# A gated attention and token-mixing MLP kernel: MLP stretches of one length, o sums kept outside PSUM, one pool of seven banks

## The chip, the core and the metric

The kernel runs on one core of one Trainium2 chip. The core has TensorE (PE in the profile, with PEld for its weight loads), VectorE (DVE), ScalarE (ACT), GpSimd (POOL) and SyncE (SP, which here issues the DMAs). TensorE writes only to PSUM, which has eight banks of 128 partitions x 512 float32 values. GpSimd does not read PSUM in this kernel: what it works on is first copied out by ScalarE or VectorE. The metric is the device time of one execution in microseconds (us), the median of several runs.

## What is computed

```python
g = sigmoid((x * gate_w).sum(-1, keepdims=True))
# attention: 32 heads of 20, one shared k and v
q = (x @ wq) as (32 heads, 2048, 20); k = x @ wk; v = x @ wv
p = softmax(q @ k.T * 20 ** -0.5)
a = concat(p @ v over the heads) @ wo
# token-mixing MLP, applied across the 2048 tokens
h = layernorm(x)                     # (2048, 640)
u = gelu(h.T @ w1 + b1)              # (640, 1728)
b = (u @ w2 + b2).T                  # (2048, 640)
return g * a + (1 - g) * b
```

x is 2048 x 640 in float32. Matrix products are computed with a high and a low part of each operand (hi x hi, hi x lo, lo x hi), so each product counts three matmuls.

## The kernel before

The program is written out in one order by hand: the scheduler is manual, so the order in the code is the order on each engine. It has a front part (layer norm, projections, about 96 us), a lead (the first seven tiles of the W1 product, mixed with the first row-max scores), the **main phase** that the change touches, and a tail of 24 o visits with the rest of the output product.

**Units and visits.** Attention runs over 32 row groups n (four blocks of 512 query rows x eight groups of four heads). Each has 16 units, one for each block kb of 128 keys. For a unit, four *scores* (`qk`, line 696: two halves b of the PE's rows x two heads pr) make four 128x512 tiles in PSUM; ScalarE takes the exp of each into an SBUF tile p (line 704). Then the *o visit* of the unit (`pv_mm`, line 732) multiplies the four p tiles with v into one PSUM bank o, each head in its own 32 partitions. Before, a group's o bank collects all 16 visits; at the end ScalarE copies it out once (line 745), and VectorE and GpSimd transpose it, divide by the sum of the exps and split it for the output product (lines 748 to 766).

**Row maxes.** The exps need the row maximum first, so the same scores are computed once more in another layout, a group or more ahead (`ms_next`, line 477), and VectorE reduces each tile to its maximum (line 480). 64 such *row-max scores* belong to each group, 2048 in all, 92 of them done in the lead.

**Fills.** The MLP and the output product are cut into matmuls of 64 rows x 320 columns (*fills*): the W1 product (`b1_jobs`, line 983), the W2 product (`b2_jobs`, line 794) and the output product for ten row blocks (`a_jobs`, line 929). All of them accumulate in one bank, g.

**Stretches.** Scores use 60 or 62 rows of one half of the PE, fills 64 rows of the other half, so two lanes run beside each other on PE. A *stretch* (`main`) issues scores of half b = k % 2 in one lane and fills in the other; `merged` mixes the two by their nominal durations (0.232 us per score, 0.147 per fill). Then come the stretch's o visits, which use all rows and all columns. Before, there are 326 stretches of 15 to 17 fills; one visit follows an even stretch and two follow an odd one. The orders are strings such as `"msmsmsssmsm"` (m a row-max score, s a score). A W1 tile takes six stretches; a W2 tile pair takes ten, for which `twin_u` copies two blocks of u to the other half of the rows so that the fills can be dealt out in five parts (`five`).

**Banks.** Six banks form a ring that scores and row-max scores take in turn (`next_bank`), one bank is o, one is g. At the start of a group, `pv_mm(swap=True)` exchanges o with the next bank of the ring. PE waits until the exp or row max of the bank's last user is done.

**Order between halves.** Fills of one stretch use one half of the rows, those of the next the other half, and both write bank g. `signal` puts a VectorE memset of one element (line 718) behind the last fill of a stretch; the first fill of the next stretch waits for it (`other_tile`).

**Small steps.** `settle` takes waiting steps (transposes, GELU steps) from lists, in the middle and at the end of a stretch; most output steps only in stretches with two visits. `w1_upto` splits weights into high and low parts on GpSimd (lines 128 and 129) some stretches ahead. `store_max` and `fetch_max` send the row maxes through DRAM into the q tile.

Of the kernel before, what the change touches and what calls it, by code (L numbers as in the profile page):

```python
# [32 lines left out]
NA = 10  # L33
EPS = 1e-5
# [5 lines left out]
def mix_kernel(ctx: ExitStack, tc: tile.TileContext, A_x, A_wq, A_wk, A_wv, A_wo,  # L40
# [51 lines left out]
    def w1_load(n):  # L92
        while len(w1raw) < min(n, len(chunks)):
# [9 lines left out]
            else:  # L103
# [3 lines left out]
                if hf == 3:  # L107
                    for h in range(2):
                        nc.sync.dma_start(out=wr[64 * (1 - h):64 * (2 - h), 2:, :],
                                          in_=B_w2[:2 * P, cols].rearrange("(c h p) s -> h p c s", c=2, h=2)[h])  # L110
# [7 lines left out]
    def w1_upto(n):  # L118
        while fetched[0] < min(n, len(chunks)):
            c = fetched[0]  # L120
            w1_load(c + 1)
            wr = w1raw[c]
            wh = w1p.tile([P, HS, P], F32R, name="wh")
            wl = w1p.tile([P, HS, P], F32R, name="wl")
            if c < 4 * PRO + 4:
                nc.scalar.activation(wh, wr, AF.Copy)
            else:
                nc.gpsimd.tensor_copy(wh, wr)
            nc.gpsimd.tensor_sub(wl, wr, f32(wh))  # L129
            w1t[c] = wh, wl  # L130
            fetched[0] += 1
            w1_load(c + 4)
# [311 lines left out]
    UC = FC + 2  # L444
    u0 = upool.tile([P, 2 * UC * HD2], F32R, name="u0")
    u_hi = [view(t, 0, UC) for t in (u0, slot[0])]
    u_lo = [view(t, UC * HD2, UC) for t in (u0, slot[0])]
    pp_pool = ctx.enter_context(tc.tile_pool(name="pp", bufs=11))
# [3 lines left out]

    row_max = {}
    mtiles = {}
    ring = []

    def next_bank():
        if not ring:
            return psl.tile([P, NB], F32, name="ml")
        ring.append(ring.pop(0))  # L460
        return ring[-1]
# [3 lines left out]
    def ms_next(b):  # L465
# [7 lines left out]
        def step():  # L473
            if n not in mtiles:
                mtiles[n] = mpool.tile([P, 16, 4], F32, name="mp")
            ms = next_bank()
            nc.tensor.matmul(ms, qmax[n][64 * b:64 * b + 60, pr, qt * P:(qt + 1) * P],  # L477
                             kst[64 * b:64 * b + 60, kq * NB:(kq + 1) * NB], start=True, stop=True)
            c = (2 * b + pr) * 4 + qt
            nc.vector.tensor_reduce(mtiles[n][:, c, kq:kq + 1], ms, axis=AX.X, op=ALU.max)  # L480
# [6 lines left out]
    def ms_done():  # L487
        n = len(row_max)
        if n < NU and min(issued) >= 32 * (n + 1):
            mm = mmpool.tile([P, 16], F32, name="mm")  # L490
            nc.vector.tensor_reduce(mm, mtiles.pop(n), axis=AX.X, op=ALU.max)
# [6 lines left out]
    def store_max(n):  # L498
        mn = row_max[n]
        mt = mpool.tile([P, 32], F32, name="mt")  # L500
        nc.vector.transpose(mt, f32(mn).rearrange("p j c -> p (j c)"))
        nc.sync.dma_start(out=m_scr[n], in_=mt)
# [10 lines left out]
    def gelu(d, fc, accs):  # L513
        both = fin.tile([P, D], F32, name="yo")
        xg, t1 = both[:, :HD2], both[:, HD2:]
        hi, lo = u_hi[d][:, fc, :], u_lo[d][:, fc, :]
        nc.scalar.activation(xg, accs[0][:, :HD2], AF.Identity, bias=bias[:, NS + fc:NS + fc + 1])

        def square():
            nc.scalar.activation(t1, xg, AF.Square)  # L520
# [5 lines left out]
        def tanh():  # L526
            nc.scalar.activation(t1, t1, AF.Tanh, scale=GC * 0.044715)
# [49 lines left out]
    with tc.tile_pool(name="psl", bufs=4, space=PSUM) as psl, \  # L577
            tc.tile_pool(name="psb", bufs=2, space=PSUM) as psb:
        at, skip, last = 0, 3, NS * PRO - 6
# [7 lines left out]
        for fc in range(PRO):  # L587
            pu = [psb.tile([P, NB], F32, name=f"pu{r}") for r in range(2)]
            for hf in range(4):
# [4 lines left out]
                for c in range(HS):  # L594
# [6 lines left out]
                    done = [max(0, min(x, last) - skip) * LEAD // (last - skip) for x in (at, at + 1)]  # L601
# [45 lines left out]
    last = {"half": None, "ins": None, "sig": None}  # L647
    flag = const.tile([1, 1], F32, name="flag")
    SYNC = mybir.DependencyInfo(mybir.DependencyClass.Sync, mybir.DependencyReason.DATA)
    sc = [0, 0]  # L650
    turn_p = [0]
    delayed = []
    X_US, F_US, EXP_US = 0.232, 0.147, 0.477
    pool, clock = [], {"now": 0.0, "act": 0.0, "dve": 0.0}

    def bank_take():
        i = min(range(len(pool)), key=lambda j: pool[j][0])
        return pool.pop(i)[1]

    def bank_give(bank, score):  # L660
        now = clock["now"]
        if score:
            clock["act"] = max(clock["act"] + EXP_US, now + 0.53)
            pool.append((clock["act"] + 0.62, bank))
        else:
            clock["dve"] = max(clock["dve"], now + 0.35) + 0.65
            pool.append((clock["dve"], bank))
# [4 lines left out]
    def next_p():  # L672
        turn_p[0] += spare[0]
        i = turn_p[0] % 14
# [14 lines left out]
    def qk(u, pr, b):  # L689
# [5 lines left out]
        s = bank_take() if pool else next_bank()  # L695
        nc.tensor.matmul(s, kst[64 * b:64 * b + 62, kb * P:(kb + 1) * P], q[64 * b:64 * b + 62, pr, :],  # L696
                         start=True, stop=True)
        if pool or clock["now"]:
            bank_give(s, True)
        p = next_p()  # L700
        ptiles[u, 2 * pr + b] = p

        def exp():
            nc.scalar.activation(p, s, AF.Exp, scale=SCALE)  # L704

        if delayed:
            delayed.append(exp)
        else:
            exp()

    def other_tile(half, ins):
        if half is not None and last["half"] not in (half, None):
            tc.add_manual_dep(ins.ins, last["sig"].ins.name, SYNC, reason="row tiles that share a bank")
        last["half"], last["ins"] = half, ins

    def signal():
        if last["ins"] is not None:
            last["sig"] = nc.vector.memset(flag, 0.0)  # L718
# [3 lines left out]
    otile = {}  # L722
    later = []

    def pv_mm(u, swap=False):
        n, kb = units[u]
        if swap:
            ring.append(otile[0])
            otile[0] = ring.pop(0)
        o = otile[0]  # L730
        for hh in range(4):
            nc.tensor.matmul(o[32 * hh:32 * hh + 32, :], v_sb[:, kb, :], ptiles.pop((u, hh)),  # L732
                             start=(kb == 0), stop=(kb == NS - 1), skip_group_check=True)
        if kb == NS - 1 and n < NU - 1:
# [3 lines left out]
            on = ev.tile([P, NB], F32, name="on")  # L738
            oh = ev.tile([P, NB], F32R, name="oh")
            ol = ev.tile([P, NB], F32R, name="ol")  # L740
            direct = spare[0]
            src = o
            if not direct:
                src = on
                nc.scalar.activation(src, o, AF.Copy)

            def turn():
                nc.vector.transpose(ot.rearrange("p c e -> p (c e)"), src)

            def scale():  # L750
                if not direct:
                    turn()
                nc.vector.reciprocal(rl, ot[:, :, DH])
# [5 lines left out]
            def back():  # L759
                nc.vector.transpose(on, ot.rearrange("p c e -> p (c e)"))  # L760
# [15 lines left out]

    FIVE = 6 * NS - (163 - 3 * (2 * FC - PRO) - 2 * NA)

    def twin_u(d):
        for t in (u_hi[d], u_lo[d]):  # L780
            h = 64 * d
            nc.sync.dma_start(out=f32(t)[64 - h:128 - h, FC:, :], in_=f32(t)[h:64 + h, :2, :])

    def b2_jobs(st):
# [12 lines left out]
        def done(d):  # L797
# [3 lines left out]
            hold["n"] = 0  # L801
            nc.scalar.activation(t[:, d * HD2:(d + 1) * HD2], hold["p"][:, :HD2], AF.Identity,
# [9 lines left out]
        def five(d):  # L812
            most = [(fc, k) for fc in range(UC) for k in range(3)]
            few = [(fc, k) for fc in range(2, FC - 1) for k in range(3)]
            parts = most[:16], few[:17], most[16:32], few[17:], most[32:]
            out = [([lambda fc=fc, k=k, h=(1 - d + i) % 2: mm(fc, k, d, h) for fc, k in p], [], [])
                   for i, p in enumerate(parts)]
# [442 lines left out]
```

## Time and profile before

| | |
|---|---|
| time, median of 3 runs | 1650.15 us (1649.99 to 1650.2) |
| span of the profiled execution | 1648.3 us |
| VectorE busy | 1428.2 us, 2721 instructions |
| ScalarE busy | 1190.8 us, 2358 instructions |
| GpSimd busy | 609.3 us, 766 instructions |
| granted TensorE clock | 9 tenths or more in every slice |
| first and last W1 fill of the main phase | 158.3 and 701.5 us |
| first and last W2 fill | 704.1 and 1399.4 us |
| first and last fill of the output product in the main phase | 1401.8 and 1573.8 us |

How to read it: the profiled execution's own time is its span; the runs' median is 1.85 us longer. A group line has the line of the code, the engine, the operation, out<-in, the shapes and the count, then busy time and the mean duration in ns, then the idle time before these instructions and what ended it. A timeline line has the start, the duration, the engine, the line and the operation. Tile names of PSUM banks (ms, s, o, g) only say where a bank was allocated: a bank called `ms` may hold a score or, before a swap, o.

### The profile page before, as it was taken

How to read it: one execution, taken by the hardware profiler on the slowest of the kernel's cores; microseconds unless marked ns; L12 is line 12 of the kernel's file. 1: busy time of each engine (PE TensorE's matmuls, PEld its weight loads, DVE VectorE, ACT ScalarE, POOL GpSimd, SP SyncE). 2: the span in 40 equal slices, each digit the busy share in tenths (PEclk: the TensorE clock that was granted, in tenths of full speed). 3: DMA queues.
4: the chain of work that ended last, by engine and by line, in shares of the span. 5: the costliest groups of instructions: out<-in, count | busy, mean ns of one | idle time of the engine just before them, and what ended most of it. 6: DMA issues, size and time to landing. Idle time of an engine off the chain costs nothing.

```text
span 1648.3 us, 38836 instructions
## 1 busy us (share of the span) xinstructions
PE 1642.6 (100%) x14877; PEld 1104.6 (67%) x14877; DVE 1428.2 (87%) x2721; ACT 1190.8 (72%) x2358; POOL 609.3 (37%) x766
## 2 busy tenths in 40 slices
PE   9999999999999999999999999999999999999999
PEld 7899666666666666666666666666666666666666
DVE  6689899999989999989998999899899999889843
ACT  4446777777777777777777777777777777777775
POOL 6568455455445555422322323232222220111120
PEclk9999999999999999999999999999999999999999
DMA  7655222222223232212222222222222221343621
GB/s 212 207 167 156 61 69 69 73 64 75 72 65 91 68 77 68 72 48 59 76 69 67 69 69 62 62 68 68 60 67 67 56 72 34 102 110 101 189 82 40
DMA packets 178527, 138.60 MB, mean 84 GB/s; under 512 B 33369, under 2 KB 144118, under 8 KB 178342
## 3 DMA queue, kind: packets, MB, share of 16 engines
q1 hardware_dynamic: 178054, 135.80, 29.8%
q8 instruction: 117, 1.92, 0.5%
q14 instruction: 68, 0.56, 0.1%
q10 hardware_dynamic: 288, 0.33, 0.1%
HBM read 102.36 MB, written 31.65 MB: 81 GB/s over the span
## 4 chain that ended last, share of the span: by engine, by line
PE 99%; DVE 1%; ACT 0%; issue 0%; DVEq 0%
PE s L732 15%; PE ms L732 11%; PE ms L477 10%; PE g L794 9%; PE s L477 8%; PE ms L696 8%; PE s L696 8%; PE g L983 7%; PE pp L298 4%; PE o L732 4%; PE o L477 3%; PE pu L599 3%; PE o L696 2%; PE g L929 2%; PE ml L477 1%; PE ms L884 1%
## 5 line engine op out<-in xcount | busy, mean ns | idle before, releaser
L480 DVE TENSOR_REDUCE mp<-ms 128x1 f32<-128x512 f32 x861 | 583.7, 685 | 59.1 <-PE ms L477 47.3
L704 ACT ACTIVATE p<-s 128x512 f32<-128x512 f32 x874 | 501.5, 604 | 183.7 <-PE s L696 176.9
L704 ACT ACTIVATE p<-ms 128x512 f32<-128x512 f32 x880 | 524.2, 605 | 125.3 <-PE ms L696 113.6
L480 DVE TENSOR_REDUCE mp<-s 128x1 f32<-128x512 f32 x795 | 532.3, 686 | 59.2 <-PE s L477 48.9
L477 PE MATMUL ms<-kst,qmx 60*128 60x512 f32 x861 | 356.6, 439 | 0.0
L696 PE MATMUL ms<-qst,kst 62*128 62x512 f32 x880 | 340.3, 398 | 0.0
L477 PE MATMUL s<-kst,qmx 60*128 60x512 f32 x795 | 335.1, 441 | 0.1
L696 PE MATMUL s<-qst,kst 62*128 62x512 f32 x874 | 330.0, 398 | 0.0
L983 PE MATMUL g<-slot,wh 64*128 64x320 f32 x1344 | 312.5, 312 | 0.0
L732 PE MATMUL s<-p,v_sb 128*32 128x512 f32 x2048 | 255.0, 600 | 0.0
L129 POOL TENSOR_TENSOR wl<-wr,wh 128x512 fp32r<-128x512 f32 x176 | 226.6, 1287 | 50.9 <-PE g L794 18.8
L477 PEld LDWEIGHTS ms<-kst,qmx 60*128 60x128 f32 x861 | 151.7, 185 | 125.6 <-ACT p L704 48.1
L983 PEld LDWEIGHTS g<-slot,wh 64*128 64x128 f32 x1344 | 222.4, 184 | 0.1
L477 PEld LDWEIGHTS s<-kst,qmx 60*128 60x128 f32 x795 | 140.9, 184 | 117.1 <-ACT p L704 49.7
L480 DVE TENSOR_REDUCE mp<-o 128x1 f32<-128x512 f32 x300 | 205.3, 684 | 13.6 <-PE o L477 12.2
L983 PE MATMUL g<-slot,wl 64*128 64x320 f32 x672 | 209.5, 312 | 0.0
L794 PE MATMUL g<-slot,wh 64*128 64x320 f32 x864 | 200.6, 313 | 0.0
L794 PE MATMUL g<-u,wh 64*128 64x320 f32 x864 | 200.4, 313 | 0.0
L704 ACT ACTIVATE p<-o 128x512 f32<-128x512 f32 x280 | 169.4, 605 | 37.5 <-PE o L696 35.2
L732 PE MATMUL ms<-p,v_sb 128*32 128x512 f32 x1536 | 191.9, 600 | 0.0
L696 PEld LDWEIGHTS s<-qst,kst 62*128 62x128 f32 x874 | 162.5, 186 | 27.3 <-issue 16.8
L696 PEld LDWEIGHTS ms<-qst,kst 62*128 62x128 f32 x880 | 162.6, 186 | 19.9 <-DVE flag L718 8.4
(257 smaller groups left out, 2900.9 us busy)
## 6 DMA issues: line engine op xcount, KB each, us to landing
wr<-in_B_w_dram SPq DMA_DIRECT2D x152, 256.0 KB
qmx<-q_scr SPq DMA_DIRECT2D x192, 80.0 KB
qst<-q_scr SPq DMA_DIRECT2D x192, 80.0 KB
slot<-o_scr SPq DMA_DIRECT2D x20, 320.0 KB
y_scr<-yo SPq DMA_DIRECT2D x16, 320.0 KB
o_scr<-oh SPq DMA_DIRECT2D x124, 40.0 KB
o_scr<-ol SPq DMA_DIRECT2D x124, 40.0 KB
q_scr<-qh SPq DMA_DIRECT2D x19, 256.0 KB
```

The source lines that it names most:

```text
L129: nc.gpsimd.tensor_sub(wl, wr, f32(wh))
L298: nc.tensor.matmul(pp, w, t, start=first and n == 0, stop=not more and n == len(steps) - 1)
L477: nc.tensor.matmul(ms, qmax[n][64 * b:64 * b + 60, pr, qt * P:(qt + 1) * P], kst[64 * b:64 * b + 60, kq * NB:(kq + 1) * NB], start=True, s ...
L480: nc.vector.tensor_reduce(mtiles[n][:, c, kq:kq + 1], ms, axis=AX.X, op=ALU.max)
L599: nc.tensor.matmul(pu[r][:, :HD2], w[rows, c, :], h[rows, st, :], start=(st == 0 and k == 0), stop=(st == NS - 1 and k == 2))
L696: nc.tensor.matmul(s, kst[64 * b:64 * b + 62, kb * P:(kb + 1) * P], q[64 * b:64 * b + 62, pr, :], start=True, stop=True)
L704: nc.scalar.activation(p, s, AF.Exp, scale=SCALE)
L732: nc.tensor.matmul(o[32 * hh:32 * hh + 32, :], v_sb[:, kb, :], ptiles.pop((u, hh)), start=(kb == 0), stop=(kb == NS - 1), skip_group_check ...
L794: other_tile(half, nc.tensor.matmul(hold["p"][:, :HD2], w[r, fc % HS, :], u[d][r, fc, :], start=(hold["n"] == 1), stop=(hold["n"] == 6 * F ...
L884: nc.tensor.matmul(acc[d, h][:, :HD2], o[r, c, :], w[r, c, d * HD2:(d + 1) * HD2], start=first, stop=last)
L929: other_tile(half, nc.tensor.matmul(hold["p"][:, :HD2], o[r, c, :], w[r, c, d * HD2:(d + 1) * HD2], start=(hold["n"] == 1), stop=(hold["n" ...
L983: other_tile(half, nc.tensor.matmul(hold["p"][:, :HD2], w[r, st % HS, :], h[d][r, st, :], start=(hold["n"] == 1), stop=(hold["n"] == 6 * NS)))
```

## The change

Six things change together.

1. W1 tiles are dealt into four stretches of 24 fills, W2 tiles into four of 20 or 21 (the last part of line 794's jobs); `five`, `twin_u` and their copies of u are gone. There are 252 stretches. Each stretch of the MLP but the first ends in two visits; in the output product the first 14 stretches end in one and 26 in two.
2. The visits of one stretch form a group of their own in PSUM: the first matmul starts a new sum, ScalarE copies the result out (to `acc` for the first of a row group, to `part` for the others) and GpSimd adds `part` to `acc`. The bank goes back into the pool after the copy. In the tail the old way stays, and VectorE adds the tail's sum to `acc` for the group that straddles the border.
3. The seven banks other than g are one pool; scores, row-max scores and visits take the bank that a small planner expects to come free first. The planner keeps times for PE, ScalarE and VectorE and decides the order in a stretch with them, starting from one string for each kind of stretch.
4. The ordering memset is gone. The exp or row max that follows the last fill waits for it too, and the first fill of the next stretch waits for that exp or row max.
5. Row-max scores are spread evenly over the stretches; a row max is stored one stretch after it is known.
6. Smaller: 12 p tiles instead of 11; the last part of a W2 tile's weights is split only where it is used; `oh` and `ol` share the space of `ot` and `acc`; tail loads are placed elsewhere.

```diff
-    def signal():
-        if last["ins"] is not None:
-            last["sig"] = nc.vector.memset(flag, 0.0)
-            tc.add_manual_dep(last["sig"].ins, last["ins"].ins.name, SYNC, reason="row tiles that share a bank")
-            last["ins"] = None
...
+    def bank_take():
+        i = min(range(len(pool)), key=lambda j: pool[j][0])
+        return pool.pop(i)[1]
+
+    def bank_give(bank, use):
+        engine, lag, us, held = USE[use]
+        start = max(clock[engine], clock["now"] + lag)
+        clock[engine] = start + us
+        pool.append((start + held, bank))
+        return start + held
...
-    def pv_mm(u, swap=False):
-        n, kb = units[u]
-        if swap:
-            ring.append(otile[0])
-            otile[0] = ring.pop(0)
+    def pv_group(us, keep=False):
+        n, kb = units[us[0]]
+        if not otile:
+            otile.append(bank_take())
         o = otile[0]
-        for hh in range(4):
-            nc.tensor.matmul(o[32 * hh:32 * hh + 32, :], v_sb[:, kb, :], ptiles.pop((u, hh)),
-                             start=(kb == 0), stop=(kb == NS - 1), skip_group_check=True)
-        if kb == NS - 1 and n < NU - 1:
+        opened = not keep or kb == 0 or us[0] == len(units) - TAIL
+        ends = kb + len(us) == NS
+        for i, u in enumerate(us):
+            for hh in range(4):
+                nc.tensor.matmul(o[32 * hh:32 * hh + 32, :], v_sb[:, kb + i, :], ptiles.pop((u, hh)),
+                                 start=opened and i == 0, stop=(i == len(us) - 1) and (ends or not keep),
+                                 skip_group_check=True)
+        if not keep:
+            begin = max(clock["act"], clock["pv"] + 0.14)
+            clock["act"] = begin + 0.477
+            pool.append((begin + 0.65, otile.pop()))
+            if kb == 0:
+                sums[0] = ev.tile([P, NB], F32, name="acc", bufs=2)
+                nc.scalar.activation(sums[0], o, AF.Copy)
+            else:
+                part = ev.tile([P, NB], F32, name="part", bufs=2)
+                nc.scalar.activation(part, o, AF.Copy)
+                nc.gpsimd.tensor_add(sums[0], sums[0], part)
+        if ends and n < NU - 1:
...
-    seq = batches([b1_jobs(*t) for t in todo], [3] * len(todo))
+    seq = batches([b1_jobs(*t) for t in todo], [2] * len(todo))
...
+    visits = [0] + [2] * (len(ph) - 4 * NA - 1)
+    left = len(units) - TAIL - sum(visits)
+    visits += [1] * (8 * NA - left) + [2] * (left - 4 * NA)
...
-    FEW = (("smsssmssmmm", "mFm"), ("smsmsmssms", "Fm"))
-    MANY = (("msmsmsssmsm", "Fm"), ("msmsmsssmsm", "Fm"))
+    PATTERN = {(2, 24): ("smsmsssmsmmsmmms", "F"), (2, 20): ("smsmssmmsmmssm", "mFs"), (2, 15): ("smsmsssmsmmss", "mFmm"),
+               (1, 15): ("msmmssms", "F"), (0, 24): ("mmmmmmmssss", "Fs")}
...
+            free = min(e for e, _ in pool)
+            tx = max(lanes[b], free) if xs else 1e9
...
+        if vs:
+            start = max([max(lanes) + DRAIN, min(e for e, _ in pool)] + [ready[v] for v in vs])
+            clock["pv"] = start + len(vs) * PV_US + ENTER
+            lanes[:] = [clock["pv"]] * 2
+            fresh[:] = [True, True]
+            pv_group(vs)
```

In `qk` and `ms_next` the exp and the row max get the dependency on the last fill that `signal` had, and they become `last["sig"]`.

More of the change, by code (lines that the diff above doesn't have):

```diff
@@ L646, in mix_kernel @@
     spare = [False]
-    last = {"half": None, "ins": None, "sig": None}
-    flag = const.tile([1, 1], F32, name="flag")
-    SYNC = mybir.DependencyInfo(mybir.DependencyClass.Sync, mybir.DependencyReason.DATA)
     sc = [0, 0]
     turn_p = [0]
[L652 to L667, printed above, removed]
+    ready = {}
     def banks_at(t):
@@ L706, in qk @@
[L706 to L709, printed above, removed]
+            e = nc.scalar.activation(p, s, AF.Exp, scale=SCALE)
+            if behind is not None:
+                tc.add_manual_dep(e.ins, behind.ins.name, SYNC, reason="row tiles that share a bank")
+                last["sig"] = e
+        exp()
     def other_tile(half, ins):
-        if half is not None and last["half"] not in (half, None):
+        if last["half"] not in (half, None):
+            assert last["ins"] is None
@@ L1085, in main @@
[L1085 to L1100 removed]
+        fs, done = list(fs), list(done)
```

264 lines of the change are left out of this document (140 added, 124 removed).

## The prediction

> **What bounds the kernel now.** I read the page first: engine shares, then the chain that ended last.
>
> ```profile
> span 1648.3 us, 38836 instructions
> ...
> PE 1642.6 (100%) x14877; PEld 1104.6 (67%) x14877; DVE 1428.2 (87%) x2721; ACT 1190.8 (72%) x2358; POOL 609.3 (37%) x766
> ...
> PE 99%; DVE 1%; ACT 0%; issue 0%; DVEq 0%
> ```
>
> The chain lies on PE for 99% of the span. A busy PE need not be a fast one, so the second look is at how a stretch repeats. In the chain in order of time, a pair of stretches (one ending in two o visits, x16, the next in one, x8) returns like this, in the first part of the main phase and in the second:
>
> ```profile
> 416.45 1.86 PE ms L732 x16
> 425.11 1.85 PE ms L732 x16
> ```
> ```profile
> 719.76 1.86 PE s L732 x16
> 724.52 1.00 PE s L732 x8
> 728.42 1.85 PE s L732 x16
> ```
>
> Both pairs take 8.66 us. Two visits cost 1.86 and one 1.00, so a stretch's scores and MLP work take (8.66 - 2.86)/2 = 2.90 us. The timeline of PE shows what those are made of:
>
> ```profile
> 251.82 1.92 PE L732 MATMUL s<-p,v_sb 128*32 128x512 f32 x16
> 253.67 0.50 PE L477 MATMUL ms<-kst,qmx 60*128 60x512 f32 x1
> 253.93 0.30 PE L983 MATMUL g<-slot,wh 64*128 64x320 f32 x1
> 254.01 0.39 PE L696 MATMUL s<-qst,kst 62*128 62x512 f32 x1
> ...
> 255.99 0.31 PE L983 MATMUL g<-slot,wl 64*128 64x320 f32 x1
> 256.15 0.50 PE L477 MATMUL ms<-kst,qmx 60*128 60x512 f32 x1
> 256.15 0.50 PE L477 MATMUL o<-kst,qmx 60*128 60x512 f32 x1
> 256.59 1.07 PE L732 MATMUL s<-p,v_sb 128*32 128x512 f32 x8
> 257.58 0.50 PE L477 MATMUL ms<-kst,qmx 60*128 60x512 f32 x1
> ```
>
> Two lanes run beside each other, one on each half of the rows. The score lane issues 11 matmuls: the second starts 0.34 us after the first, the tenth after that at 256.15, so 9 steps take 2.14, 0.238 each. The MLP lane issues 16 fills, 0.147 apart ((255.99 - 253.93)/14), and one row-max score. Both end at 256.15; the visits begin 0.44 later. So a stretch costs 0.34 + 0.44 of start and end, whatever it holds, and the visits another 0.13: two take 253.67 - 251.82 = 1.85, one 257.58 - 256.59 = 0.99, hence 0.86 per visit. Fewer, longer stretches save these constants. VectorE and ScalarE, which free the score banks, were read next:
>
> ```profile
> 253.81 0.60 ACT L745 ACTIVATE on<-s 128x512 f32<-128x512 f32 x1 [1.07 <-PE s L732]
> 254.44 0.60 ACT L704 ACTIVATE p<-s 128x512 f32<-128x512 f32 x1
> 254.94 0.59 ACT L704 ACTIVATE p<-ms 128x512 f32<-128x512 f32 x1
> ```
> ```profile
> 254.21 0.69 DVE L480 TENSOR_REDUCE mp<-ms 128x1 f32<-128x512 f32 x1 [0.98 <-PE ms L477]
> 254.82 0.68 DVE L480 TENSOR_REDUCE mp<-s 128x1 f32<-128x512 f32 x1
> 255.41 0.68 DVE L480 TENSOR_REDUCE mp<-ms 128x1 f32<-128x512 f32 x1
> ```
>
> An exp follows the one before by 0.48 to 0.50 us, a row max by 0.60; the first of each starts 0.43 to 0.54 after its matmul. Here ScalarE also holds an o copy ahead of the exps, started 0.14 after the visits, and the stretch under it takes 256.59 - 253.67 = 2.92, as the others do.
>
> **Part by part.** *The o copies and sums.* Of 31 groups with a copy, the change goes to 251: 31 first copies and 220 partial ones, each with a GpSimd add. Rows that price them:
>
> ```profile
> L480 DVE TENSOR_REDUCE mp<-ms 128x1 f32<-128x512 f32 x861 | 583.7, 685 | 59.1 <-PE ms L477 47.3 <-PE g L794 4.9
> ...
> L129 POOL TENSOR_TENSOR wl<-wr,wh 128x512 fp32r<-128x512 f32 x176 | 226.6, 1287 | 50.9 <-PE g L794 18.8 <-ACT wh L126 13.4 <-PE s L477 3.5
> ...
> L128 POOL CAST wh<-wr 128x512 fp32r<-128x512 f32 x144 | 88.0, 611 | 195.1 <-PE g L794 99.7 <-PE ms L696 42.2 <-PE s L696 36.1
> ...
> L766 POOL TENSOR_TENSOR ol<-on,oh 128x512 fp32r<-128x512 f32 x31 | 39.9, 1286 | 1.4
> ...
> L748 DVE STREAM_TRANSPOSE ot<-on 128x512 f32<-128x512 f32 x30 | 21.1, 702 | 0.0
> ...
> L718 DVE MEMSET flag<- 1x1 f32 x326 | 19.2, 59 | 0.0
> ```
>
> ScalarE: 221 more copies x 0.49 = 108 us; with eight exps and a copy, a stretch asks 9 x 0.49 = 4.4 us of ScalarE in about 5.6. GpSimd: 220 adds x 1.286 = 283 us. In the first part a pair of stretches (11.7 us after the change) then asks two weight splits of 0.611 + 1.287, two adds of 1.286, and about 3 us of GELU and output steps: 9.4 us, 80%. Nothing on PE waits for the sum within its own stretch, and the weights are split a pair ahead, so I cost the adds at nothing; if GpSimd fell two groups behind, the copy would wait for its buffer and the exps queued behind it with it (a rival below).
>
> *The memset.* 59 ns each, starting inside the tail of the last row max: nothing on the path. The first fill now waits for the last exp instead, which is done some 1.1 us after its matmul, under 1.85 us of visits; its cover is the visits, and without them it would cost up to 0.7.
>
> *The stretches.* From the kernel's own order: 84 stretches of W1 work instead of 126, 128 of W2 instead of 160, 40 of the output product as before: 252 for 326. Two visits now follow 237 of them, one follows 14. The lanes hold: W1, 16 scores against 24 fills; W2, 14 scores against a row max, 20 fills (21 in 32 stretches) and a score; output product, 13 against m, 15 fills, m, m (26 stretches), and 8 against 15 fills (14 stretches).
>
> W1: 0.34 + 14 x 0.238 = 3.67 to the last score, + 0.34 when only one lane ends last (a little under the 0.44 of the quoted stretch) = 4.0 us. W2 by the MLP lane: 0.34 + 20 x 0.147 = 3.28 to the closing score, 3.62 to the visits; 21 fills 3.77.
>
> *The banks.* Scores and visits take whichever of seven banks comes free, and PE issues in order, so a wait for a bank stops both lanes. How long a bank is held is shown by the output product, where the ring of before runs dry:
>
> ```profile
> 1448.54 0.73 PE L477 MATMUL s<-kst,qmx 60*128 60x512 f32 x2
> ...
> 1450.07 0.39 PE L696 MATMUL s<-qst,kst 62*128 62x512 f32 x1
> ...
> 1450.45 0.50 PE L696 MATMUL s<-qst,kst 62*128 62x512 f32 x1
> ...
> 1451.66 1.92 PE L732 MATMUL ms<-p,v_sb 128*32 128x512 f32 x16
> ```
> ```profile
> 1449.11 1.89 DVE L480 TENSOR_REDUCE mp<-s 128x1 f32<-128x512 f32 x3 [0.32 <-PE s L477]
> ```
>
> The step to 1450.45 takes 0.38 instead of 0.24. That score takes the bank of the second row max, which began at 1449.71, so a bank returns to PE 0.74 us after its row max begins. By the same count with these numbers, through a W2 stretch: row maxes begin at 0.54, 1.15, 1.75, 2.36, 2.96, exps at 0.62, 1.1, 1.6, 2.1, 2.6; each later score finds its bank 0.1 to 0.3 us ahead, and the visits' bank, the fifth row max's, returns at 2.96 + 0.74 = 3.70. So 3.70 instead of 3.62, and 3.80 with 21 fills. W1 is less dense and waits for nothing (4.0). The two-visit output stretches pack 16 scores into 2.94 us: the same count gives 3.68. One-visit: 0.1 + 15 x 0.147 + a score + 0.34 = 2.65.
>
> *The sum.* Before: 63 pairs x 8.66 + 80 pairs x 8.66 + 32 extra fills x 0.15, and for the output product
>
> ```profile
> L929 PE MATMUL g<-slot x600: 299/306/415, 1401.8 to 1573.8; 64*128 64x320 f32 x150
> ```
>
> 172.0 + 2.5 to the end of its last visits: 545.6 + 697.6 + 174.5 = 1417.7; the first stretch has no visit, -1.0. After: 84 x 5.85 + 96 x 5.55 + 32 x 5.65 + 26 x 5.53 + 14 x 3.64 = 1399.8, less 1.85 for the first. The difference is -18.8 us. About 10 of it are visit entries and 8 start-and-end constants; a good part of the latter goes back because the lanes are less even (W1: 3.8 us of scores beside 3.5 of fills). The odd work (two transposes of 0.70 and small steps on VectorE per row group, GELU steps on ScalarE) falls on longer bursts with less slack; between nothing and 0.3 us per group of 31 for VectorE and again for ScalarE, I take 5 us. Span 1648.3 - 18.8 + 5 = 1634.5; the runs' median is 1.85 over the span of the profiled execution, so **1636 us**.
>
> **Rivals.**
> *No bank wait at all*: W2 at 3.62 and 3.77, output at 3.37, no odd work: 8.6 + 8.1 + 5 less, 1614 to 1618. For it: the ring of six never stalled in W1 and W2. Against: my count leaves the visits' bank no slack.
>
> *Bank waits in every stretch (slower)*: place, the last scores and the visits; price, the 0.14 us stall of the quoted output stretch in each of 236 two-visit stretches, +34 us, 1670. It decides from 0.06 us per stretch on, since that eats the 14 us gained. For it: bursts of 16 instead of 12 scores between pauses, ScalarE with a copy first, and margins of 0.1 us in an order fixed beforehand. Against: a seventh bank, and the stretch with a copy above ran undisturbed.
>
> *VectorE is the bound*: it is 91% busy in the MLP parts:
>
> ```profile
> 167.00:699.00 532.00, 532.00 (x4920) 347.50 (x4916) 483.87 (x915) 407.42 (x810) 273.12 (x356) 1.00 0.27 71
> 703.00:1399.00 696.00, 696.00 (x6421) 454.87 (x6415) 629.76 (x1194) 513.36 (x1007) 182.34 (x227) 1.00 0.23 64
> ```
>
> (third figure after the widths: 483.87 and 629.76 of VectorE). If a row max really took its 0.685 us, eight and 0.25 of odd work would need 5.73 per stretch: +0.16 in W2 and +0.2 in the output product, 26 us, 1662. Against it: consecutive ones start 0.60 apart, and VectorE's idle time ends on PE (47.3 of 59.1 us in its first row). The Trainium skill, Perfetto Trace Analysis, Identifying the Most-Contended Engine, tells one to take the engine with the highest occupancy as the bottleneck and not to trust matmul busy time, which speaks for this rival; the start-to-start rows speak against it.
>
> *GpSimd falls behind* in W1: at 80%, a lost microsecond per pair would be 42 us, 1678.
>
> *Nothing gained*: the uneven lanes and small waits take the 19 us back, 1647 to 1653.
>
> **How the numbers follow.** Forecast (1624 to 1645) 0.51; no bank wait 0.09; bank waits 0.20; VectorE 0.05; GpSimd 0.04; nothing gained 0.11, of which 0.08 lies within 0.2% (3.3 us, about what a measurement can tell), 0.02 below and 0.01 above. Faster 0.51 + 0.09 + 0.02 = 0.62; same 0.08; slower 0.20 + 0.05 + 0.04 + 0.01 = 0.30. The range reaches from the edge of the no-wait case to just under the full bank price: 1617 to 1668; the forecast's own is 1624 to 1645.
>
> **What would show it.** Right: visits (x16) 5.85 us apart in W1, 5.55 to 5.65 in W2; VectorE without the memset; a GpSimd add per stretch, each done before the next copy. Wrong: gaps between scores over 0.24 inside a stretch, or visits that begin more than 0.45 us after the last score (banks); row maxes back to back through the visits (VectorE); copies that start later than 0.14 us after the visits (GpSimd's buffers).

## The result, and the profile after

The changed kernel takes 1635.84 us (median, 1635.39 to 1636.21), the kernel before beside it 1650.16. The ratio is 0.9912, 95% interval 0.9898 to 0.9926: 14.3 us less, against 14 forecast. The profiled execution has a span of 1634.0 us, against 1634.5 in the sum.

The page of the changed kernel, its span, its engines and the engines of its chain of waits:

```profile
span 1634.0 us, 39357 instructions
...
PE 1623.5 (99%) x14877; PEld 1133.6 (69%) x14877; DVE 1395.2 (85%) x2396; ACT 1304.3 (80%) x2579; POOL 873.2 (53%) x986
...
PE 94%; ACT 5%; issue 1%; DVE 0%; DVEq 0%; ACTq 0%
```

PE still sets the end, with the same 14877 matmuls, but 5% of the chain has moved to ScalarE: there are now moments when a matmul waits for an exp. ScalarE has 221 instructions more, GpSimd 220 more, VectorE 325 fewer.

The chain in order of time, in the first part and the second (start, length, what):

```profile
414.19 1.85 PE ms L735 x16
420.00 1.90 PE s L735 x16
425.92 1.92 PE s L735 x16
...
749.91 1.85 PE s L735 x16
755.47 1.85 PE o L735 x16
```

Two visits return every 5.8 to 5.9 us in the first part and after 5.56 in the second; the prediction asked for 5.85, and 5.55 to 5.65. (A row of the chain can start up to 0.1 us behind the same row of the timeline.)

To compare whole phases I summed, from PE's timeline, every stretch from its first matmul to its first visit, and the visits to the next first matmul. W1 is the first part (b1), W2 the second (b2), from the third stretch on:

| | by the sum, us | measured, us |
|---|---|---|
| first two stretches, change against before | +2.2 | +3.1 |
| W1: before / after | 536.9 / 479.7 | 537.0 / 479.8 |
| W2: before / after | 697.6 / 713.6 | 697.8 / 718.4 |
| output product: before / after | 174.5 / 194.7 | 174.3 / 193.5 |
| in all | -18.8 | -14.3 |

The phases of before and W1 after come out within 0.2 us. The difference of 4.5 us in all, for which the sum had put down 5 us of odd work without a place, lies in W2 (+4.8) and the start (+0.9); the output product gives 1.2 back. Mean time before the visits is 4.00 us in W1, 3.73 and 3.83 in W2 stretches of 20 and 21 fills; visits take 1.855.

PE's timeline of one W2 stretch (start, length, engine and line, operation):

```profile
749.84 1.92 PE L735 MATMUL s<-p,v_sb 128*32 128x512 f32 x16
751.70 0.50 PE L700 MATMUL o<-qst,kst 62*128 62x512 f32 x1
...
752.03 0.30 PE L802 MATMUL g<-u,wl 64*128 64x320 f32 x1
...
755.05 0.42 PE L700 MATMUL s<-qst,kst 62*128 62x512 f32 x1
755.40 1.92 PE L735 MATMUL o<-p,v_sb 128*32 128x512 f32 x16
```

And VectorE under its last part:

```profile
754.07 0.68 DVE L494 TENSOR_REDUCE mp<-ms 128x1 f32<-128x512 f32 x1
754.67 0.68 DVE L494 TENSOR_REDUCE mp<-o 128x1 f32<-128x512 f32 x1
```

The stretch lasts 755.40 - 751.70 = 3.70, the figure of the prediction. The visits go into bank `o`, whose row max began at 754.67, 2.97 after the stretch: 0.73 later the bank is PE's. That is the count of the prediction to a hundredth; whether it is also the reason was a question for the experiments (it is not alone).

The partial sum, on ScalarE, on GpSimd, and all adds in the page's groups:

```profile
751.88 0.60 ACT L747 ACTIVATE part<-s 128x512 f32<-128x512 f32 x1 [0.30 <-PE s L735]
```
```profile
752.58 1.30 POOL L748 TENSOR_TENSOR acc<-acc,part 128x512 f32<-128x512 f32 x1
```
```profile
L748 POOL TENSOR_TENSOR acc<-acc,part 128x512 f32<-128x512 f32 x220 | 284.6, 1294 | 349.0 <-ACT part L747 344.4
```

The copy starts 0.18 after the visits' end (751.70), where the prediction had read 0.14 and named a later start as a sign against it; the median is 0.20 in W1 and 0.19 in W2. The add follows when the copy is done, 1.294 long where 1.286 was assumed, and 344 of the 349 us that GpSimd idles ahead of adds are spent waiting for a copy: over the whole GpSimd keeps up.

W1 has one stretch in four that is longer: 4.14 against 3.94 to 3.96. One of these, on PE and on ScalarE:

```profile
445.19 0.50 PE L700 MATMUL ms<-qst,kst 62*128 62x512 f32 x1
...
448.81 0.40 PE L700 MATMUL s<-qst,kst 62*128 62x512 f32 x1
449.32 1.92 PE L735 MATMUL ms<-p,v_sb 128*32 128x512 f32 x16
```
```profile
447.79 0.64 ACT L709 ACTIVATE p<-s 128x512 f32<-128x512 f32 x1
448.26 0.51 ACT L549 ACTIVATE yo<-yo 128x320 f32<-128x320 f32 x1
448.62 0.64 ACT L709 ACTIVATE p<-ms 128x512 f32<-128x512 f32 x1
```

Line 549 is the tanh of a GELU. The next exp would have followed at about 448.26, one exp's step behind 447.79; it starts at 448.62. The visits go into a bank named `ms`, as that exp's is, and begin 0.51 after the last score: 449.32 is 0.70 after the exp's start. That the tanh is the cause was put to the test below.

The start of the main phase, on PE and on VectorE:

```profile
164.18 0.41 PE L986 MATMUL g<-slot,wh 64*128 64x320 f32 x1 [1.00 <-ACT p L709]
...
167.89 1.92 PE L735 MATMUL ms<-p,v_sb 128*32 128x512 f32 x16
...
170.16 0.50 PE L700 MATMUL ms<-qst,kst 62*128 62x512 f32 x1
```
```profile
169.42 0.68 DVE L494 TENSOR_REDUCE mp<-o 128x1 f32<-128x512 f32 x1
```

The first stretch has no visits, so nothing hides the exp behind its last fill, for which the next first fill now waits: idle 1.00. After the first visits PE resumes 2.27 us after they began instead of 1.85, just behind a late row max (169.42 + 0.68 = 170.10), which carries the order there.

### The profile page after: what moved, and what is told of

Same layout as the page of the kernel before. It is cut to its first block, busy times and chain, and to the rows that moved or that the text cites. A ratio compares the mean times of both kernels' runs of the same rounds, so it can differ in the third digit from the quotient of the medians.

```text
span 1634.0 us, 39357 instructions
## 1 busy us (share of the span) xinstructions
PE 1623.5 (99%) x14877; PEld 1133.6 (69%) x14877; DVE 1395.2 (85%) x2396; ACT 1304.3 (80%) x2579; POOL 873.2 (53%) x986
## 4 chain that ended last, share of the span: by engine, by line
PE 94%; ACT 5%; issue 1%; DVE 0%; DVEq 0%; ACTq 0%
PE s L735 14%; PE g L802 11%; PE ms L735 11%; PE ms L700 9%; PE s L700 8%; PE g L986 7%; PE ms L488 6%; PE s L488 6%; PE pp L296 4%; ACT p L709 4%; PE o L735 4%; PE pu L621 3%; PE o L700 3%; PE g L931 3%; PE o L488 2%; PE ml L488 1%
## 5 line engine op out<-in xcount | busy, mean ns | idle before, releaser
L494 DVE TENSOR_REDUCE mp<-ms 128x1 f32<-128x512 f32 x842 | 554.7, 682 | 65.8 <-PE ms L488 51.8
L494 DVE TENSOR_REDUCE mp<-s 128x1 f32<-128x512 f32 x823 | 542.9, 682 | 66.1 <-PE s L488 55.1
L748 POOL TENSOR_TENSOR acc<-acc,part 128x512 f32<-128x512 f32 x220 | 284.6, 1294 | 349.0 <-ACT part L747 344.4
L700 PE MATMUL ms<-qst,kst 62*128 62x512 f32 x894 | 352.8, 411 | 0.0
L700 PE MATMUL s<-qst,kst 62*128 62x512 f32 x861 | 340.4, 411 | 0.0
L488 PE MATMUL ms<-kst,qmx 60*128 60x512 f32 x842 | 328.9, 410 | 0.0
L488 PE MATMUL s<-kst,qmx 60*128 60x512 f32 x823 | 320.3, 409 | 0.5 <-DVE yo L544 0.5
L127 POOL TENSOR_TENSOR wl<-wr,wh 128x512 fp32r<-128x512 f32 (+1 forms) x176 | 218.1, 1239 | 29.4 <-ACT wh L124 9.7
L494 DVE TENSOR_REDUCE mp<-o 128x1 f32<-128x512 f32 x291 | 198.1, 681 | 19.4 <-PE o L488 15.2
L735 PE MATMUL ms<-p,v_sb 128*32 128x512 f32 x1512 | 182.3, 598 | 1.0
L709 ACT ACTIVATE p<-o 128x512 f32<-128x512 f32 x280 | 173.1, 618 | 10.7 <-PE ms L735 4.2
```

The source lines that it names most:

```text
L127: nc.gpsimd.tensor_sub(wl[:, :nv], wr[:, :nv], f32(wh[:, :nv]))
L494: r = nc.vector.tensor_reduce(mtiles[n][:, c, kq:kq + 1], ms, axis=AX.X, op=ALU.max)
L709: e = nc.scalar.activation(p, s, AF.Exp, scale=SCALE)
L735: nc.tensor.matmul(o[32 * hh:32 * hh + 32, :], v_sb[:, kb + i, :], ptiles.pop((u, hh)), start=opened and i == 0, stop=(i == len(us) - 1) a ...
L748: nc.gpsimd.tensor_add(sums[0], sums[0], part)
```

## The experiments

In the first group (four kernels) the copies, the adds and the memset were taken apart; in the second the banks and the row maxes; the third tries what came out of them. Every kernel is compared with the kernel before (1650.07 to 1650.35 in these runs), and with the changed kernel's 1635.84.

**No partial copies and adds.**

```diff
-                part = ev.tile([P, NB], F32, name="part", bufs=2)
-                nc.scalar.activation(part, o, AF.Copy)
-                nc.gpsimd.tensor_add(sums[0], sums[0], part)
+                pass
```

> The kernel after without the 220 partial o copies on ScalarE and their GpSimd adds (the partial sums of a row group but the first are left out of the output). Same order on PE. My theory (the copies lie beside PE; they only push the exps of a stretch back by up to 0.2 us): 1628 to 1636 us. Rival (the copies hide a larger gain): 1620 or less.

Measured: 1631.73 us, ratio 0.9889 (0.9872 to 0.9905), 4.1 less than the changed kernel and inside the range of the theory. (The output of this kernel and of the next lacks these sums.)

**The copies kept, the adds away.**

```diff
-                nc.gpsimd.tensor_add(sums[0], sums[0], part)
```

> The kernel after with the copies but without the 220 GpSimd adds (only the first visits of a row group reach the output). My theory (nothing waits for the sums): 1634.5 to 1637. Rival (GpSimd at 80% in the W1 part holds up splits, GELU steps or copy buffers): 1630 or less.

Measured: 1632.51 us, ratio 0.9893. The 220 adds cost 3.3 us, between what the two theories gave, and the copies, with 108 us of ScalarE, cost 0.8. By phases the adds cost 1.9 us in W1, 0.6 in W2, 0.4 at the start. "At nothing" was too little, but GpSimd is not what paces the kernel. The long W1 stretch falls from 4.14 to 4.06, which is 1.6 of the 1.9 us; the others hardly change. ScalarE and PE of the long stretch shown above, which here starts at 443.70:

```profile
443.83 0.60 ACT L747 ACTIVATE part<-s 128x512 f32<-128x512 f32 x1 [1.29 <-PE s L735]
...
447.08 0.64 ACT L709 ACTIVATE p<-ms 128x512 f32<-128x512 f32 x1
```
```profile
447.77 1.92 PE L735 MATMUL ms<-p,v_sb 128*32 128x512 f32 x16
```

The copy starts 0.13 after the visits before it, with the adds 0.19 (445.38). From the copy to this exp ScalarE has no idle time, so the exp starts 3.38 after the stretch's start instead of 3.43, and the visits follow it by 0.69 here and by 0.70 there. Without the adds the median copy starts 0.14 after the visits in W1 and W2, with them 0.20 and 0.19. Why a copy that an add will read starts later is not shown, nor where the rest of the 3.3 us is lost.

**The changed kernel with the memset back.**

```diff
-            behind, last["ins"] = last["ins"], None
+            behind = None
...
+    def signal():
+        last["sig"] = nc.vector.memset(flag, 0.0)
+        tc.add_manual_dep(last["sig"].ins, last["ins"].ins.name, SYNC, reason="row tiles that share a bank")
+        last["ins"] = None
...
                     issue(1 - b, F_US, fs.pop(0), tf)
+                    if not fs:
+                        signal()
```

> The kernel after with the ordering memset on VectorE put back: behind the last fill of a stretch, the first fill of the next one waits for it, exps and row maxes no longer carry that order. My theory (hidden under the visits): 1634 to 1639. Rival (its removal is a good part of the gain): 1642 or more.

Measured: 1643.59 us, ratio 0.996 (0.9945 to 0.9975). The rival was right: 7.8 us, more than half of what the change gains. The stretches of W1 are 1.1 us shorter in all, but the visits now take 2.00 to the next fill instead of 1.855 (11.7 us more; W1 as a whole +10.7); the start is 1.8 us shorter and one-visit output stretches lose a wait of 0.09. VectorE and PE of this kernel in W1:

```profile
442.38 1.28 DVE L494 TENSOR_REDUCE mp<-ms 128x1 f32<-128x512 f32 x2
443.60 0.06 DVE L725 MEMSET flag<- 1x1 f32 x1
```
```profile
441.75 1.92 PE L742 MATMUL o<-p,v_sb 128*32 128x512 f32 x16
443.83 0.38 PE L993 MATMUL g<-slot,wh 64*128 64x320 f32 x1 [0.16 <-POOL wl L127]
```

The memset takes 0.06 us and costs 0.14, because it stands behind eight row maxes. In the longer stretch VectorE is still reducing when the visits end (441.75 + 1.85 = 443.60); the first fill comes 0.17 after the memset is done. (The row names GpSimd's weight split as the releaser of this fill; the visits take over 1.90 in 76 of the 82 stretches, and the memset in place of the other carrier is all that this kernel changes.)

**The kernel before without its memset**: the first exp or row max after the last fill carries the order, as in the change, nothing else.

```diff
+            behind, last["ins"] = last["ins"], None
             r = nc.vector.tensor_reduce(mtiles[n][:, c, kq:kq + 1], ms, axis=AX.X, op=ALU.max)
+            if behind is not None:
+                tc.add_manual_dep(r.ins, behind.ins.name, SYNC, reason="row tiles that share a bank")
+                last["sig"] = r
...
-        fill = [(F_US, f) for f in fs] + [(0.0, f) for f in [signal] + done]
+        fill = [(F_US, f) for f in fs] + [(0.0, f) for f in done]
```

The exp in `qk` gets the same lines.

> The kernel before with the memset removed and the order carried by the exp or row max behind the last fill, nothing else changed. My theory: 1648 to 1651, no change. Rival (the memset's removal is the gain): 1636 to 1643.

Measured: 1657.87 us, ratio 1.0047 (1.0032 to 1.0062): neither theory, 7.7 us slower. W2 is 8.6 us longer, in two stretches of every ten (by 0.36 and 0.18); the start is 0.6 shorter. The place, on ScalarE and PE:

```profile
812.40 0.63 ACT L811 ACTIVATE yo<-g,b2g,og_half 128x320 f32<-128x320 f32 x1
812.90 0.62 ACT L710 ACTIVATE p<-ms 128x512 f32<-128x512 f32 x1
```
```profile
812.09 1.06 PE L741 MATMUL ms<-p,v_sb 128*32 128x512 f32 x8
813.08 0.49 PE L479 MATMUL ms<-kst,qmx 60*128 60x512 f32 x1
813.58 0.49 PE L700 MATMUL o<-qst,kst 62*128 62x512 f32 x1
```

The same place in the kernel before, on VectorE and PE:

```profile
812.45 0.06 DVE L718 MEMSET flag<- 1x1 f32 x1
```
```profile
811.71 1.07 PE L732 MATMUL ms<-p,v_sb 128*32 128x512 f32 x8
812.70 0.49 PE L477 MATMUL ms<-kst,qmx 60*128 60x512 f32 x1
812.71 0.56 PE L794 MATMUL g<-slot,wh 64*128 64x320 f32 x2
```

At the end of a block of fills ScalarE takes the block's sum out of PSUM (`yo`) first, and the exp that carries the order is queued behind it: it ends at 813.52. One visit is the only cover, it ends at 813.08, and the MLP lane starts half a microsecond late. With the memset, on a VectorE that was ahead, the fills started with the score. So the price of the order is the place of its carrier in its engine's queue, and the cheap carrier is another one before the change than after it.

**Six banks instead of seven** (the seventh is held back until after the main phase).

```diff
-    pool.append((0.0, ps_o.tile([P, NB], F32, name="o")))
+    pool.append((lanes[0], ps_o.tile([P, NB], F32, name="o")))
```

In the second line the bank is added where the pool is extended after the main phase. The kernel before had six banks for scores and one for the visits; this one has six for both.

> The kernel after with six banks in the pool of the main phase instead of seven, as many as the ring of before had; the order on PE may shift, since the planner sees the same six. My theory (by the count of bank releases a W2 stretch would have to wait for its closing score until about 3.7 instead of 3.28 us, the visits 0.3 later; W1 0.1, output 0.4): 1670 to 1700, slower than before. Rival (the seventh bank is not needed, the fewer stretches alone make the gain): 1636 to 1645.

Measured: 1715.77 us, ratio 1.0396 (1.0381 to 1.0412), 80 us more than with seven and beyond what was expected. Stretches take 4.27 in W1, 4.13 in W2, two-visit stretches of the output product 4.10. PE and VectorE in W2:

```profile
771.71 0.39 PE L488 MATMUL s<-kst,qmx 60*128 60x512 f32 x1
771.97 0.50 PE L700 MATMUL s<-qst,kst 62*128 62x512 f32 x1
772.40 1.92 PE L735 MATMUL ms<-p,v_sb 128*32 128x512 f32 x16
```
```profile
770.64 1.28 DVE L494 TENSOR_REDUCE mp<-s 128x1 f32<-128x512 f32 x2
```

The second of those two row maxes begins 0.60 after the first, at 771.24, and the score at 771.97 comes 0.73 later: here the last score follows VectorE's release of its bank.

**Seven banks, taken in the order in which they are given back** and not by the planner's estimate of when they come free.

```diff
-        i = min(range(len(pool)), key=lambda j: pool[j][0])
+        i = 0
```

> The kernel after where a bank is taken in the order in which banks were given back in the program, not the one expected free first. My theory (in W2 the closing score falls on the bank of the fifth row max, 0.4 us late, in W1 less): 1655 to 1680. Rival (any seven banks in turn do): 1634 to 1642.

Measured: 1712.43 us, ratio 1.0377 (1.0361 to 1.0392), 77 us more than the changed kernel and, again, beyond what was expected. The stretches of W1 and W2 take 4.27 and 4.13, as with six banks; two-visit output stretches 3.77. 5.9 of the 77 us lie in the tail, where banks are taken in the same way. The likely reason, not tested by itself: exps and row maxes return their banks from two queues, so the oldest bank need not be the first one free. The seventh bank is worth something only with the choice.

**Row max over half of its columns** (the other 256 of each 512 are left out).

```diff
-            r = nc.vector.tensor_reduce(mtiles[n][:, c, kq:kq + 1], ms, axis=AX.X, op=ALU.max)
+            r = nc.vector.tensor_reduce(mtiles[n][:, c, kq:kq + 1], ms[:, :NB // 2], axis=AX.X, op=ALU.max)
```

> The kernel after with every row max of the main phase and the lead taken over 256 of 512 columns (the other half of the keys is left out of the row maximum), same order on PE. My theory (what is left of waits in W2 and the output product are banks held by row maxes: 0.1 us in W2, 0.35 in two-visit output stretches): 1614 to 1624. Rival (PE alone sets the time): 1633 to 1637. Rival (VectorE is the bound outright): under 1610.

Measured: 1627.8 us, ratio 0.9863: 8.0 less than the changed kernel, less than was expected. Between the two profiled executions, which lie 8.6 apart, 2.4 come at the start, 5.4 in W2 and 1 in W1. In W2 the mean falls from 3.73 to 3.71 with 20 fills and from 3.83 to 3.75 with 21, but the median of the 20-fill stretches stays at 3.71. PE and VectorE of one of them:

```profile
747.14 0.49 PE L700 MATMUL o<-qst,kst 62*128 62x512 f32 x1
...
750.42 0.49 PE L700 MATMUL s<-qst,kst 62*128 62x512 f32 x1
750.84 1.92 PE L735 MATMUL o<-p,v_sb 128*32 128x512 f32 x16
```
```profile
749.40 0.41 DVE L494 TENSOR_REDUCE mp<-o 128x1 f32<-128x256 f32 x1
```

Bank `o` is free a microsecond before the visits, and they still begin 750.84 - 747.14 = 3.70 after the start. The closing score stands at 3.28, where the prediction's count of fills put it, and the visits come 0.42 later, not 0.34: both lanes end with a score here, as in the stretch quoted in the prediction, where it was 0.44. In the changed kernel the weight load of the same closing score starts 3.28 after the stretch too, and the visits 0.42 after it:

```profile
754.98 0.18 PEld L700 LDWEIGHTS s<-qst,kst 62*128 62x128 f32 x1
755.40 0.16 PEld L735 LDWEIGHTS o<-p,v_sb 128*32 128x32 f32 x8 [0.24 <-DVE mp L494]
```

Two paths of 3.70 tie, and freeing the bank leaves the other.

So the 5.4 us of W2 do not come from the visits' bank in the usual stretch: the 76 stretches with 20 fills that took under 3.74 give back 0.03 us together. 2.9 us come from the 32 stretches with 21 fills, and 1.9 from 16 with 20 fills, one per row group, that took 3.77. One of the 16 in the changed kernel, on PE's weight loads and on VectorE:

```profile
687.57 0.18 PEld L488 LDWEIGHTS o<-kst,qmx 60*128 60x128 f32 x1 [0.15 <-DVE mp L494]
```
```profile
684.93 0.25 DVE L767 RECIPROCAL rl<-ot 128x16 f32<-128x16 f32 x1
...
686.84 0.68 DVE L494 TENSOR_REDUCE mp<-o 128x1 f32<-128x512 f32 x1
```

The MLP lane's last row-max score waits for a bank whose row max began 0.73 earlier (686.84 to 687.57), and the fill behind it in PE's order starts no sooner (687.58). In all 16, and in 30 of the 32 with 21 fills, this weight load comes 0.73 to 0.74 after a row max began. In the 16 the row maxes start 0.06 to 0.13 late, behind a step of the o output (the reciprocal); in those with 21 fills they start at their usual times.

**W2's scores set earlier in the row** (two scores of the lane move ahead of row maxes).

```diff
-    PATTERN = {(2, 24): ("smsmsssmsmmsmmms", "F"), (2, 20): ("smsmssmmsmmssm", "mFs"), (2, 15): ("smsmsssmsmmss", "mFmm"),
+    PATTERN = {(2, 24): ("smsmsssmsmmsmmms", "F"), (2, 20): ("smsmssmsmsmmsm", "mFs"), (2, 15): ("smsmsssmsmmss", "mFmm"),
```

> The kernel after with two scores of the W2 order moved forward past a row-max score each (s m s m s s m s m s m m s m for s m s m s s m m s m m s s m), an attempt at a faster version. My theory (the visits find an exp's bank at about 3.66 instead of a row max's at 3.70): 1630 to 1635. Rival (the order is not what the visits wait for): 1635 to 1637; worse if the row maxes bunch at the end: up to 1645.

Measured: 1636.31 us, ratio 0.9914 (0.9897 to 0.993): no change, as the rival had it. The order on PE differs in all 128 W2 stretches, and W2 takes 718.4 us as before the edit. In the stretch read (763.49) the visits still follow a row max, which begins 2.97 after the start as before, and not an exp as was meant. It fits the tie, since no order within the lane moves its end, but tells nothing more.

**The memset only where the other carrier is late**: in the first two stretches and in those with one visit.

```diff
-            behind, last["ins"] = last["ins"], None
+            behind, last["ins"] = (None, last["ins"]) if own[0] else (last["ins"], None)
...
+        own[0] = k <= 1 or len(vs) < 2
...
+                    if own[0] and not fs:
+                        signal()
```

> The changed kernel with the memset put back in the first two stretches and in the stretches that end in one visit only; everywhere else the first score or row max after the last fill carries the order, as in the change. Theory (what carries the order costs by its place in the queue of its engine: the memset loses 0.14 us where two visits follow eight row maxes, and gains where VectorE's queue is short, 1.8 us at the start and 0.10 us in each one-visit stretch): 1632.0 to 1634.5 us, with W1 stretches unchanged at 4.00 + 1.85. Rival (the gains of the kernel with the memset everywhere came from its other schedule, not from the carrier): 1635 to 1638 us.

Measured: 1632.99 us (1632.88 to 1633.45), ratio 0.9897. As expected: the start is 1.6 us shorter, the output product 1.0, W1 keeps its 4.00 + 1.855. So the cost of the kernel with the memset everywhere was the carrier in W1, and its gain elsewhere the carrier as well.

**The tanh one place later in the GELU's chain**, so that it falls behind the last exp of its stretch.

```diff
-            chain.extend((square, cube_p, None, tanh, prod_p, high_p))
+            chain.extend((square, cube_p, None, None, tanh, prod_p, high_p))
```

> The changed kernel with the tanh of each W1 GELU one place later in its chain, so that ScalarE meets it behind the last exponential of that stretch and not between two of them. Theory (the second of every four W1 stretches is 0.18 us longer than the others because the tanh delays the exponentials that free the banks of its closing scores and of the visits): that stretch falls from 4.14 to about 3.96 us, 20 of them, 1631 to 1634 us. Rival (the 0.18 us come from the GpSimd and VectorE work of that stretch or of the next): the stretch keeps 4.1 us, 1635 to 1637 us.

Measured: 1632.21 us (1631.86 to 1632.38), ratio 0.9892, as expected. The long stretch falls from 4.14 to 3.97, W1 from 479.8 to 476.6 us.

**Both edits.**

> The two edits together (memset in the first two and in the one-visit stretches, tanh one place later). Theory: they touch different stretches and add up, 1628.5 to 1632 us, faster than both kernels of this study. Rival (the planner's choice of banks shifts with either edit and gives part of it back): 1632 to 1636 us.

Measured: 1629.73 us (1629.41 to 1629.92), ratio 0.9876 (0.986 to 0.9893): 6.1 less than the changed kernel, inside the range of the theory and the fastest that computes everything. By themselves the two edits gave 2.9 and 3.6. ScalarE at the place of the tanh:

```profile
446.05 0.66 ACT L710 ACTIVATE p<-o 128x512 f32<-128x512 f32 x1
446.55 0.51 ACT L550 ACTIVATE yo<-yo 128x320 f32<-128x320 f32 x1
447.94 0.60 ACT L752 ACTIVATE acc<-ms 128x512 f32<-128x512 f32 x1 [0.88 <-PE ms L743]
```

The tanh now stands in the idle time of ScalarE under the visits, ahead of the copy, and delays neither.

Not tried: W1 in more, shorter stretches with the rest of the change, and the kernel before with copies and sums. So the gain of the fewer stretches alone is worked out from the phases, not isolated.

## Why the prediction was right

*What bounds the kernel; the constants of a stretch.* Right. PE's chain of scores, fills and visits set the time, and 324 stretches from the third on became 250: 1409.1 to 1391.7 us in those phases, 17.4 less, 8.9 of it in visits and 8.6 in the stretches, where the prediction had 10 and 8. That the fewer entries and ends save this much is argued from these phases, not isolated by a run.

*W1 at 4.0.* Right as a mean, and in part by luck: three of four stretches take 3.95, a little under the count, and the fourth 4.14, where the prediction saw no wait. Moving the tanh showed the reason: the bank of the visits waits for an exp that the tanh delays, and the visits begin 0.50 after the last score, which the prediction had named as a sign of bank waits.

*W2 at 3.70 and 3.80.* Right in size (medians 3.71 and 3.83), but the step that put 0.08 down to the bank of the fifth row max named one of two causes. The wait is there, to a hundredth, and with it gone the end of two lanes takes as long. Therefore the rival without bank waits had a wrong floor: its 3.62 took 0.34 from the last score to the visits, which holds where one lane ends alone. With 21 fills the wait that counts is not at the visits but at the last row-max score, 0.09 us.

*The output product at 3.68 and 2.65.* Two visits: 3.72, right. One visit: 2.39. The sum had put a closing score and its 0.34 behind the fills; in the trace the visits follow the last fill by 0.23, and no score stands between. The visits there take 1.09 instead of 0.99, which the carrier explains (0.996 with the memset). The shorter stretches offset part of what W2 takes more.

*The odd work, 5 us.* The size came out (4.5), its place was guessed, and that the sum is met so closely is luck: W2 and the start take 5.7 more than counted, the output product 1.2 less, and in W1 the tanh (3.2 us) fills what the count had too much. Of the 5.4 us that halving the row maxes removed from W2, the 1.9 behind the reciprocal can be put down to odd work on VectorE; the 2.9 in the stretches with 21 fills are a bank wait that the count had not placed.

*The adds at nothing.* Mis-sized: 3.3 us. Wrong was that only PE's own wait for a sum was looked at; with adds the copies start about 0.06 us later, and where ScalarE is full this reaches the visits.

*The memset at nothing.* Right for the memset of the kernel before, where the memset ends inside the visits, and wrong for what it says of the change. Two effects were left out. With longer stretches a memset behind eight row maxes would have cost 7.8 us, so replacing it is a part of the gain. And the new wait was priced with visits as cover, "without them up to 0.7"; the sum then forgot that the first stretch has no visits and that others have only one (1.00 of idle time at the start). In the kernel before the same replacement costs 7.7 us.

*The rivals.* Bank waits in every stretch did not happen, but that rival was the nearest to deciding: with six banks, or with seven in the wrong order, the stretches pay 0.27 us in W1 and 0.37 in W2 on the mean, two to nearly three times the 0.14 that the prediction took from one row of before, and the kernel is 62 to 65 us slower than before, not 20. VectorE as the bound has fallen: it asked for 5.73 us per W2 stretch, which takes 5.61 (718.4 / 128), and half the row max saved 8 us in all. The rule in the Trainium skill, Perfetto Trace Analysis, Identifying the Most-Contended Engine, would have pointed there; the runs do not agree with it: half the row max takes VectorE's busy time from 1395.2 to 913.7 us and the kernel down by 8. GpSimd behind has fallen with the 3.3 us that the adds cost, where it asked for 42.

## What to carry to other kernels

In these kernels an instruction that only carries an order cost what its engine's queue held ahead of it, beyond what the visits cover, and not its own 0.06 us: look at which queue is shortest at that place, stretch by stretch, and look again when the stretches change length. When buffers are few, count when each comes back from the instruction that reads it last, and choose by that; here one bank more and the choice were worth 80 and 77 us, more than five times the change itself. Before freeing a resource that a wait names, ask what ends next: of two paths of 3.70 us, shortening one gave nothing.

## What the runs showed that was not expected

A PSUM bank came back to PE 0.73 us after its row max began in two kernels with quite different waits (754.67 to 755.40 with seven banks, 771.24 to 771.97 with six) and 0.74 in the kernel before; the weight loads of the 46 stretches above give 0.73 to 0.74 as well. For an exp it was 0.70 (448.62 to 449.32) and 0.69 without the adds (447.08 to 447.77). A tanh of 0.51 us on 320 columns delayed the next exp by 0.36 only, since ScalarE's rows overlap like VectorE's.
